# Value products of batch 0 on two column tiles of the array

## The chip, the cores and the metric

The kernel runs on one core of one Trainium2 chip. The metric is the device time of one execution in microseconds (us). TensorE (PE) does the matrix products; VectorE (DVE), ScalarE (ACT) and GpSimd (POOL) work elementwise; SyncE (SP) issues most of the DMAs. PEld names PE's loads of the stationary operand, which stand in rows of their own.

## The reference

Attention with a decay, for 8 batches and 8 heads of 576 tokens with 64 channels, and then a feed-forward layer with a softplus over all 4608 tokens.

```python
scores = scale * np.matmul(q, k.transpose(0, 1, 3, 2))
cum = np.cumsum(np.log(np.clip(f, 0.0001, 1.0)), axis=-1)
scores = np.where(causal, -1000000000.0, scores + cum[:, :, :, None] - cum[:, :, None, :])
attn = np.exp(scores - np.max(scores, axis=-1, keepdims=True))
attn = attn / (np.sum(attn, axis=-1, keepdims=True) + 1e-09)
x = np.matmul(attn, v)                     # 8 x 8 x 576 x 64, then 4608 x 512
h = x @ w_in                               # 512 -> 2048
g = np.maximum(h, 0.0) + np.log1p(np.exp(-np.abs(h)))
out = g @ w_out                            # 2048 -> 512
```

## The kernel before, in words

The program is one long list of operations that a planner (class Plan) puts in order. Each operation names the engines that may do it with a cost in us, what it comes after, and the buffers that it takes. The planner walks through the list with a clock for each engine, takes whatever can start first, and lets the engine with the better end do it. So a changed cost, or an operation split or merged, can change the order of the neighbours and the engine on which a copy runs. The order is fixed when the program is built; on the chip each engine works down its own list and waits where a semaphore tells it to.

Until the first product of the down projection (tile "acc") the planner also writes filler matmuls for PE (tile "fill", function fill_gap, line 1377): wherever its clock sees PE idle for more than 0.5 us it puts in matmuls of 128 columns for 0.7 of that time. They compute nothing that is used. They are instructions like others, and PE works through them whether or not it would have waited.

Attention goes job by job. Batch 0 is "plain": float32 operands, with one matmul in the program being two records in the trace. Its jobs are four pairs of heads for queries 0 to 255 (function first) and then eight single heads for queries 256 to 575 (function rest). All other batches (function whole) split each operand into a high and a low part and take two or three matmuls (lines 763, 764 and 918). A plain job computes scores (line 761, tile s), minima on DVE (line 768), exponentials on ACT (line 788), normalises, turns the weights with PE transposes (line 859, tile b), copies them out of PSUM (tile p; ACT or DVE), and multiplies them with the values (line 912, tile o). The output lies transposed: 64 channels on the partitions, queries in the columns, so the stationary operand is 128 keys by 64 channels and half of the array's columns are used. A copy by ACT or DVE then puts it into x, the feed-forward layer's input; that is the helper's line 213, as are all copies.

The value products are made by output(gi), one call for each range of queries and head in "groups". A pair has two groups, one for each head: two products each (256 and 128 columns) into a PSUM bank of their own. A single head has one group of 320 queries and five products, with 320, 320, 320, 192 and 64 columns, since the later keys are seen by the later queries only. In a list "banks" stand the parts of the turned weights: each entry is a first key, a range of queries and a chunk of v.

Weights arrive as 64-bit numbers and are converted in the first 150 us by ACT, POOL and DVE (lines 441 to 465), then split into high and low parts (lines 508 to 534). Block 0 of the feed-forward layer, 256 tokens, is also plain (lines 1057 and 1180); later blocks use lines 1076 and 1161. All PSUM banks of the attention come from one tag, "att", with four buffers.

Of the kernel before, what the change touches and what calls it, by code (L numbers as in the profile page):

```python
# [216 lines left out]
def tile_decay_attention_softplus_ffn(  # L217
# [18 lines left out]
    B, D, H, _, S = qkT.shape  # L236
    NT, DM = out.shape
    DFF = w_in.shape[1]
    P = 128
# [41 lines left out]
    T = {}  # L281
# [288 lines left out]
    def rest(h):  # L570
        return dict(
            b=0, heads=[h], q=(256, S), k=(0, S), nv=NCH,
            tiles=[(q0, n, 0, 2 + i, 0) for i, (q0, n) in enumerate(QR)],
            banks=[[(0, 256, S, 0), (384, 384, S, 3)], [(128, 256, S, 1), (512, 512, S, 4)],
                   [(256, 256, S, 2)]],
            groups=[(256, S, h, 256)],
        )

    x_of, x_taken = {}, {}
# [6 lines left out]
    def attention(job):  # L586
# [237 lines left out]
        def weights(bi):  # L824
# [70 lines left out]
            for key, lo, hi, vc, at in spans:  # L895
                parts.append((lo, hi, bi, vc, at, box, ready, small))

        def output(gi):
            g0, g1, h, tok = groups[gi]
            g, j = h // 2, h % 2  # L900
            todo = sorted(
                (p for p in parts if p[0] < g1 and p[1] > g0), key=lambda p: (max(p[0], g0) > g0, p[2])
            )
            box, last = {}, []
            for i, (lo, hi, bi, vc, at, pbox, ready, small) in enumerate(todo):
                a, z = max(lo, g0), min(hi, g1)

                def values(e, i=i, a=a, z=z, vc=vc, o=at + a - lo, pbox=pbox, xs="h" if small else "hl"):
                    if i == 0:
                        box["ps"] = bank("att", f"o{n}_{gi}")  # L910
                    if plain:
                        e.matmul(  # L912
                            box["ps"][0:64, a - g0 : z - g0], st["vr"][:, vc, :],
                            pbox["p"][:, o : o + z - a], start=i == 0, stop=i == len(todo) - 1,
                        )
                        return
                    for x in xs:
                        e.matmul(  # L918
                            box["ps"][:, a - g0 : z - g0], st["vhl"][:, vc, :],
                            pbox[x][:, o : o + z - a],  # L920
                            start=i == 0 and x == "h", stop=i == len(todo) - 1 and x == xs[-1],
                        )

                on = on_pe32(z - a) if plain else on_pe(z - a, len("h" if small else "hl"))
                op = add(
                    on, values, after=ready + last + st["V"],
                    takes=("att",) if i == 0 else (),
                )
                last = [op]
                used[bi].append(op)  # L930
            st.setdefault("ends", []).extend(last)
            w = g1 - g0


            def to():
                if b not in x_of:
                    x_of[b] = buf("x32", [P, NCC, S], f"x32_{b}")
                return x_of[b][64 * j : 64 * j + 64, g, tok : tok + w]

            def shift(e):  # L940
                copy(e, to(), box["ps"][64 - 64 * j : 128 - 64 * j, 0:w])

            def put(e):
                if plain:
                    copy(e, to(), box["ps"][0:64, 0:w])
                    return
                e.tensor_add(to(), box["ps"][64 * j : 64 * j + 64, 0:w], to())

            needs = last + x_taken.get(b, [])
            takes = () if b in x_taken else ("x32",)  # L950
            if plain:
                d = c = add([on_act(w, psum=True), on_dve(w)], put, after=needs, takes=takes)
            else:
                c = add(on_act(w, psum=True), shift, after=needs, takes=takes)
                d = add(on_dve(w), put, after=[c])
            x_taken.setdefault(b, [c])
            puts = [d]
            wrote.setdefault(b, []).append((tok, tok + w, d))
            give("att", puts)
            if gi == len(groups) - 1:  # L960
                if plain:
                    give("T0", st["scores"])
                    if number == nplain - 1:
                        give("x32", cum_used)
                    give(st["vtag"], st["ends"])
                    for bi, ops in used.items():
                        give(tags[bi], ops)
                else:
                    give("T", st["scores"])
                    give("vhl", st["ends"])  # L970
                    for bi, ops in used.items():
                        if banks[bi][0][:3] == (0, 0, 64):
                            give("ph64", ops)
                        else:
                            give("ph", ops)
                            give("pl", ops)

        def loads():
            (load32 if plain else load)()
# [3 lines left out]
            load=loads, prepare=None if plain else prepare, fin=finish_stats,  # L983
            s=[lambda ti=ti: stat_tile(ti) for ti in range(nt)],
            w=[lambda bi=bi: weights(bi) for bi in range(len(banks))],
            o=[lambda gi=gi: output(gi) for gi in range(len(groups))],
        )


# [481 lines left out]
```

## Time and profile before

| what | before |
|---|---|
| time, median of 3 runs | 1186.32 us (1185.65 to 1186.48) |
| profiled execution, its own time | 1184.87 us |
| its span, first to last instruction | 1183.1 us |
| granted clock of TensorE, mean | 0.999 |
| busy: PE, DVE, ACT, POOL | 1170.2, 809.2, 832.3, 131.0 us |
| value products of batch 0 (line 912) | 112 records, from 18.6 to 141.0 us |
| first "acc" product (line 1180) | 82.06 us |

The span is what the views show; the execution's own time has 1.8 us around it. Rows of PE overlap: the printed length of a matmul holds the time that its result takes to leave the array, so the cost of a row in a stream is read from its start to the next start. That PE is 99% busy therefore doesn't mean that PE streams columns for 99% of the time.

### The profile page before, as it was taken

How to read it: one execution, taken by the hardware profiler on the slowest of the kernel's cores; microseconds unless marked ns; L12 is line 12 of the kernel's file. 1: busy time of each engine (PE TensorE's matmuls, PEld its weight loads, DVE VectorE, ACT ScalarE, POOL GpSimd, SP SyncE). 2: the span in 40 equal slices, each digit the busy share in tenths (PEclk: the TensorE clock that was granted, in tenths of full speed). 3: DMA queues.
4: the chain of work that ended last, by engine and by line, in shares of the span. 5: the costliest groups of instructions: out<-in, count | busy, mean ns of one | idle time of the engine just before them, and what ended most of it. 6: DMA issues, size and time to landing. Idle time of an engine off the chain costs nothing.

```text
span 1183.1 us, 19397 instructions
## 1 busy us (share of the span) xinstructions
PE 1170.2 (99%) x6112; PEld 967.3 (82%) x6112; DVE 809.2 (68%) x2013; ACT 832.3 (70%) x1991; POOL 131.0 (11%) x145
## 2 busy tenths in 40 slices
PE   8999999999999999999999999999999999999998
PEld 6766678888888888888888888888888888888887
DVE  7977898987787678767776678667866773223322
ACT  5887779877876787677867877778767773444543
POOL 5312011100110011110000101001011010000000
PEclk9999999999999999999999999999999999999999
DMA  8856756655566555655566546656566433211210
GB/s 243 242 163 180 205 155 180 152 147 147 155 181 186 165 152 166 181 177 158 150 198 187 151 138 202 178 147 172 152 185 175 139 106 120 89 47 44 89 54 36
DMA packets 120759, 180.30 MB, mean 152 GB/s; under 512 B 22945, under 2 KB 80305, under 8 KB 120657
## 3 DMA queue, kind: packets, MB, share of 16 engines
q1 hardware_dynamic: 120640, 179.05, 52.9%
q8 instruction: 49, 0.80, 0.3%
q14 instruction: 54, 0.43, 0.1%
q10 hardware_dynamic: 16, 0.01, 0.0%
HBM read 109.98 MB, written 35.95 MB: 123 GB/s over the span
## 4 chain that ended last, share of the span: by engine, by line
PE 90%; DVE 5%; ACT 2%; issue 1%; DMA 1%; POOL 0%; SPq 0%; DVEq 0%; POOLq 0%; ACTq 0%
PE acc L1161 30%; PE h L1076 30%; PE b L859 8%; PE o L918 6%; PE s L764 3%; PE s L763 3%; PE h L1057 2%; PE acc L1180 2%; PE o L912 2%; PE s L761 1%; DVE s L768 1%; ACT p L788 1%; DMA sti<-in_w_in 1%; DVE pl L878 1%; DVE h L1123 0%
## 5 line engine op out<-in xcount | busy, mean ns | idle before, releaser
L1076 PE MATMUL h<-xh,wih 128*128 128x512 f32 (+1 forms) x576 | 228.9, 400 | 0.2 <-DVE gl L1131 0.2
L788 ACT ACTIVATE p<-s,negm 128x288 f32<-128x288 f32 (+7 forms) x384 | 183.0, 479 | 64.6 <-DVE negm L768 62.6
L1076 PE MATMUL h<-xl,wih 128*128 128x512 f32 (+1 forms) x576 | 216.5, 379 | 0.0
L768 DVE CUSTOM_DVE_ANT_0 s<-s,cmask 128x288 f32<-128x288 f32 (+5 forms) x320 | 137.7, 439 | 89.0 <-PE s L764 82.5
L1123 DVE SCALAR_TENSOR_TENSOR h<-h,e 128x512 f32<-128x512 f32 x136 | 95.7, 704 | 129.1 <-ACT e L1115 128.2
L812 POOL TENSOR_SCALAR p<-p,rsum 64x64 f32<-64x64 f32 (+4 forms) x83 | 91.7, 1113 | 759.9 <-DVE rsum L801 329.4
L1109 ACT ACTIVATE e<-h 128x512 f32<-128x512 f32 x144 | 85.9, 597 | 118.8 <-PE h L1076 115.8
L1161 PE MATMUL acc<-woh_dt_float32r,gh 128*128 128x512 f32 x376 | 153.2, 407 | 0.0
L1076 PE MATMUL h<-xh,wl 128*128 128x512 f32 (+1 forms) x576 | 148.6, 380 | 0.0
L1161 PE MATMUL acc<-woh_dt_float32r,gl 128*128 128x512 f32 x376 | 147.2, 392 | 0.0
L1161 PE MATMUL acc<-wol_dt_float32r,gh 128*128 128x512 f32 x376 | 146.9, 391 | 0.0
L878 DVE TENSOR_TENSOR pl<-b,ph 128x512 fp32r<-128x512 f32 x168 | 110.9, 665 | 19.6 <-ACT ph L213 16.3
L1131 DVE TENSOR_TENSOR gl<-h,gh 128x512 fp32r<-128x512 f32 x136 | 93.5, 687 | 42.7 <-ACT gh L213 40.3
L1076 PEld LDWEIGHTS h<-xh,wl 128*128 128x128 f32 x576 | 104.8, 188 | 21.5
L1076 PEld LDWEIGHTS h<-xh,wih 128*128 128x128 f32 x576 | 108.7, 189 | 15.4 <-PE b L859 0.4
L1076 PEld LDWEIGHTS h<-xl,wih 128*128 128x128 f32 x576 | 108.8, 189 | 14.5
L859 PE MATMUL b<-ident,p 128*128 128x128 f32 (+1 forms) x728 | 118.3, 270 | 1.1 <-POOL p L812 0.6
L213 ACT CAST ph<-b 128x512 fp32r<-128x512 f32 (+2 forms) x170 | 82.7, 487 | 47.9 <-PE b L859 40.9
L213 ACT CAST gh<-h 128x512 fp32r<-128x512 f32 x111 | 65.2, 587 | 57.4 <-DVE h L1123 38.0
L810 ACT ACTIVATE p<-p,rsum 128x192 f32<-128x192 f32 (+7 forms) x193 | 96.6, 555 | 6.1 <-DVE rsum L801 5.8
L859 PEld LDWEIGHTS b<-ident,p 128*128 128x128 f32 (+1 forms) x728 | 86.7, 138 | 16.4 <-issue 3.5
L763 PE MATMUL s<-T 128*64 128x64 f32 x336 | 97.6, 303 | 1.2 <-issue 1.1
(152 smaller groups left out, 2248.5 us busy)
## 6 DMA issues: line engine op xcount, KB each, us to landing
wl<-wil_d SPq DMA_DIRECT2D x72, 512.0 KB
T<-T SPq DMA_DIRECT2D x224, 144.0 KB
raw<-in_qkT SPq DMA_DIRECT2D x112, 144.0 KB
g_d<-gh SPq DMA_DIRECT2D x84, 128.0 KB
g_d<-gl SPq DMA_DIRECT2D x84, 128.0 KB
vr<-in_vR SPq DMA_DIRECT2D x64, 160.0 KB
out<-ob SPq DMA_DIRECT2D x36, 256.0 KB
sto<-in_w_out SPq DMA_DIRECT2D x11, 512.0 KB
```

The lines of the kernel that those rows point to most:

```text
L213: (e.tensor_copy if hasattr(e, "tensor_copy") else e.copy)(out, in_)
L763: e.matmul(o, qA[:, q0:end], kA[:, a:z], start=True, stop=False)
L768: e.tensor_tensor_reduce(out=box["o"], in0=box["o"], in1=cmask[0:n_q, right - w : right], scale=-0.125, scalar=m0 if i else 3.0e38, op0=AL ...
L788: e.activation(o, box["o"], AF.Exp, bias=m1, scale=-1.0, accum_out=acc)
L810: e.activation(a, a, AF.Copy, scale=f_)
L812: e.tensor_scalar(a, a, f_, None, ALU.mult)
L859: e.transpose(box["ps"][0 : x.shape[1], at : at + one.shape[1]], x, one)
L878: e.tensor_sub(box["l"], box["ps"][:, 0:w], box["h"].bitcast(F32))
L1076: e.matmul(o, l, r, start=m == 0, stop=m == 11)
L1123: e.scalar_tensor_tensor(h, h, 0.0, box["e"], ALU.max, ALU.add)
L1131: e.tensor_sub(box["l"], box["t"], box["h"].bitcast(F32))
L1161: e.matmul(st["acc", tt], l, r[fc], start=first and m == 0, stop=last and m == 2,)
```

## The change

A new function, output_tiled, takes the place of output(gi) in all plain jobs. The result of a job is put into one PSUM bank, with its first group on partitions 0 to 63 and its second on partitions 64 to 127; tile_position=(0, 64 * r) puts the stationary operand of group r into the left or the right 64 columns of the array. In a pair the two groups are the two heads. A single head gets two groups, queries 256 to 447 and 448 to 575. The products of both groups are written in turns and form one planner operation for each step (a step is a product of both heads in a pair, and a part of the turned weights in a single head), whose cost is counted as that of the wider group alone. A pair is copied out by one copy of 128 partitions, a single head by two copies of 64 partitions. output(gi) loses its plain branches.

```diff
@@ -573,7 +573,7 @@
             tiles=[(q0, n, 0, 2 + i, 0) for i, (q0, n) in enumerate(QR)],
             banks=[[(0, 256, S, 0), (384, 384, S, 3)], [(128, 256, S, 1), (512, 512, S, 4)],
                    [(256, 256, S, 2)]],
-            groups=[(256, S, h, 256)],
+            groups=[(256, 448, h, 256), (448, S, h, 448)],
         )
...
@@ -895,6 +895,75 @@
+        def output_tiled():
+
+            todo = []
+            for g0, g1, *_ in groups:
+                here = [x for x in parts if x[0] < g1 and x[1] > g0]
+                todo.append(sorted(here, key=lambda x: (max(x[0], g0) > g0, x[2])))
+            if pair:
+                steps = [[[x] for x in both] for both in zip(*todo)]
+            else:
+                steps = [[[x for x in ts if x[2] == bi] for ts in todo] for bi in range(len(banks))]
+            box, last, left = {}, [], [len(ts) for ts in todo]
+            for i, step in enumerate(steps):
+                mms, need, cols = [], [], []
+                for r, (ts, (g0, g1, *_)) in enumerate(zip(step, groups)):
+                    cols.append(0)
+                    for k, (lo, hi, bi, vc, at, pbox, ready, _) in enumerate(ts):
+                        a, z = max(lo, g0), min(hi, g1)
+                        left[r] -= 1
+                        mms.append((k, r, a - g0, z - g0, vc, pbox, at + a - lo, i + k == 0, not left[r]))
+                        cols[-1] += z - a
+                        need += ready
+
+                def values(e, i=i, mms=sorted(mms, key=lambda m: m[:2])):
+                    if i == 0:
+                        box["ps"] = bank("att", f"o{n}")
+                    for _, r, a, z, vc, pbox, o, start, stop in mms:
+                        e.matmul(
+                            box["ps"][64 * r : 64 * r + 64, a:z], st["vr"][:, vc, :],
+                            pbox["p"][:, o : o + z - a], start=start, stop=stop,
+                            tile_position=(0, 64 * r),
+                        )
+
+                op = add(
+                    on_pe32(max(cols)), values, after=need + last + st["V"],
+                    takes=("att",) if i == 0 else (),
+                )
+                last = [op]
+                for ts in step:
+                    for x in ts:
+                        used[x[2]].append(op)
+            st["ends"] = last
+
+            g, j = heads[0] // 2, heads[0] % 2
+            outs = [(0, P, *groups[0])] if pair else [(64 * r, 64, *x) for r, x in enumerate(groups)]
+            puts = []
+            for r, rows, g0, g1, _, tok in outs:
+                w = g1 - g0
+
+                def put(e, r=r, rows=rows, tok=tok, w=w):
+                    if b not in x_of:
+                        x_of[b] = buf("x32", [P, NCC, S], f"x32_{b}")
+                    to = x_of[b][64 * j : 64 * j + rows, g, tok : tok + w]
+                    copy(e, to, box["ps"][r : r + rows, 0:w])
+
+                takes = () if b in x_taken else ("x32",)
+                d = add(
+                    [on_act(w, psum=True), on_dve(w)], put, after=last + x_taken.get(b, []), takes=takes,
+                )
+                x_taken.setdefault(b, [d])
+                puts.append(d)
+                wrote.setdefault(b, []).append((tok, tok + w, d))
+            give("att", puts)
+            give("T0", st["scores"])
+            if number == nplain - 1:
+                give("x32", cum_used)
+            give(st["vtag"], st["ends"])
+            for bi, ops in used.items():
+                give(tags[bi], ops)
+
...
@@ -908,12 +977,6 @@
                     if i == 0:
                         box["ps"] = bank("att", f"o{n}_{gi}")
-                    if plain:
-                        e.matmul(
-                            box["ps"][0:64, a - g0 : z - g0], st["vr"][:, vc, :],
-                            pbox["p"][:, o : o + z - a], start=i == 0, stop=i == len(todo) - 1,
-                        )
-                        return
...
-                on = on_pe32(z - a) if plain else on_pe(z - a, len("h" if small else "hl"))
+                on = on_pe(z - a, len("h" if small else "hl"))
...
@@ -983,7 +1032,7 @@
             w=[lambda bi=bi: weights(bi) for bi in range(len(banks))],
-            o=[lambda gi=gi: output(gi) for gi in range(len(groups))],
+            o=[output_tiled] if plain else [lambda gi=gi: output(gi) for gi in range(len(groups))],
         )
```

The change moves instructions, since the planner's costs and operations are others. Three places follow; a number at the end of a name is a buffer's.

PE, third pair of heads (o_0, o_1 and o are value products, p the turned weights, b transposes, fill the fillers, s scores), before:

```order
42 L912 MATMUL o_0_418<-p_0_402,vr_153 64x256
43 L912 MATMUL o_0_418<-p_0_402,vr_153 64x128
44 L859 MATMUL b_1_428<-ident,p_640_95 128x128 x3
45 L1377 MATMUL fill<-cmask 128x128 x3
46 L912 MATMUL o_1_445<-p_1_435,vr_153 64x256
47 L912 MATMUL o_1_445<-p_1_435,vr_153 64x128
48 L1377 MATMUL fill<-cmask 128x128 x3
```

and after:

```order
42 L859 MATMUL b_1_401<-ident,p_640_95 128x128 x3
43 L1426 MATMUL fill<-cmask 128x128 x4
44 L924 MATMUL o_420<-p_0_397,vr_153 64x256
45 L924 MATMUL o_420<-p_1_412,vr_153 64x256
46 L924 MATMUL o_420<-p_0_397,vr_153 64x128
47 L924 MATMUL o_420<-p_1_412,vr_153 64x128
48 L1426 MATMUL fill<-cmask 128x128 x11
```

The four products stand together, behind the transposes of both heads, and take turns.

PE, third single head of batch 0, the last one ahead of the first "acc", before:

```order
133 L859 MATMUL b_2_794<-ident,p_640_95 128x128
134 L912 MATMUL o_0_803<-p_0_780,vr_635 64x320
135 L912 MATMUL o_0_803<-p_1_798,vr_635 64x320
136 L912 MATMUL o_0_803<-p_2_805,vr_635 64x320
137 L912 MATMUL o_0_803<-p_0_780,vr_635 64x192
138 L912 MATMUL o_0_803<-p_1_798,vr_635 64x64
139 L1377 MATMUL fill<-cmask 128x128 x4
140 L761 MATMUL s_0_0_840<-T_72 64x320
```

and after:

```order
137 L761 MATMUL s_2_288_803<-T_73 128x288
138 L924 MATMUL o_808<-p_0_781,vr_642 64x192
139 L924 MATMUL o_808<-p_0_781,vr_642 64x128
140 L924 MATMUL o_808<-p_0_781,vr_642 64x64
141 L924 MATMUL o_808<-p_0_781,vr_642 64x128
142 L924 MATMUL o_808<-p_1_786,vr_642 64x192
143 L924 MATMUL o_808<-p_1_786,vr_642 64x128
144 L924 MATMUL o_808<-p_1_786,vr_642 64x64
145 L924 MATMUL o_808<-p_2_797,vr_642 64x192
146 L924 MATMUL o_808<-p_2_797,vr_642 64x128
147 L1426 MATMUL fill<-cmask 128x128 x13
148 L761 MATMUL s_0_0_867<-T_72 64x320
```

Five products became nine, and the filler behind them 13 rows' worth where there were 4. Behind the value products of the last pair the fillers number 36 (in four places) and were 21 (in six).

DVE, up to the weights of the last pair (wih and wil are high and low parts of w_in, negm the minima), before:

```order
106 L213 CAST wih<-woh_dt_float_326 128x512
107 L213 CAST wih<-woh_dt_float_449 128x512
108 L768 ISA s_2_288_497,negm_75<-s_2_288_497,cmask,negm_75 128x288
109 L768 ISA negm_75 128x1
110 L213 COPY x_0_282<-o_0_501 64x256
111 L213 COPY p_1_518<-b_1_512 128x384
```

and after, at the same place of the last pair (its second transposes wait for row 97):

```order
97 L812 TENSOR_SCALAR p_640_100<-p_640_100,rsum_90 128x256
98 L512 TENSOR_TENSOR wil_477<-woh_dt_float_216,wih 128x512
99 L768 ISA s_0_0_467,negm_75<-s_0_0_467,cmask 64x320
100 L768 ISA negm_75 64x1
101 L512 TENSOR_TENSOR wil_489<-woh_dt_float_256,wih 128x512
102 L465 SCALAR_TENSOR_TENSOR woh_dt_float_446<-ti_440,woh_dt_float_446 128x512
```

The copy of the turned weights has gone to ACT, and the two low parts of line 512, which stood ahead of the last pair's weights, stand behind them. From the first down product of the third block on (line 1161, row 951 of PE before and 978 now), PE's rows are the same in both programs.

More of the change, by code (lines that the diff above doesn't have):

```diff
@@ L943, in put @@
             def put(e):
-                if plain:
-                    copy(e, to(), box["ps"][0:64, 0:w])
-                    return
                 e.tensor_add(to(), box["ps"][64 * j : 64 * j + 64, 0:w], to())
@@ L950, in output @@
             takes = () if b in x_taken else ("x32",)
[L951 to L955, printed above, removed]
+            c = add(on_act(w, psum=True), shift, after=needs, takes=takes)
+            d = add(on_dve(w), put, after=[c])
             x_taken.setdefault(b, [c])
@@ L960, in output @@
             if gi == len(groups) - 1:
[L961 to L976, printed above, removed]
+                give("T", st["scores"])
+                give("vhl", st["ends"])
+                for bi, ops in used.items():
+                    if banks[bi][0][:3] == (0, 0, 64):
+                        give("ph64", ops)
+                    else:
+                        give("ph", ops)
+                        give("pl", ops)
         def loads():
```

## The prediction, made before the changed kernel ran

> **What bounds the kernel now.** First the page: the engines' busy time, the chain that ended last, and the group of the products that are edited.
>
> ```profile
> span 1183.1 us, 19397 instructions
> PE 1170.2 (99%) x6112; PEld 967.3 (82%) x6112; DVE 809.2 (68%) x2013; ACT 832.3 (70%) x1991; POOL 131.0 (11%) x145
> PE 90%; DVE 5%; ACT 2%; issue 1%; DMA 1%; POOL 0%; SPq 0%; DVEq 0%; POOLq 0%; ACTq 0%
> ```
>
> PE is busy all the time and the chain runs on it for 90% of the span. So PE time saved where PE is the chain shortens the kernel, one for one until another engine is late. The edited products end early, so the second view is the table of stretches, for all instructions and then for the filler matmuls alone (line 1377).
>
> ```profile
> 20.00:43.00 23.00, 21.46 (x123) 15.79 (x122) 22.44 (x59) 19.68 (x51) 11.05 (x14) 0.93 0.88 274
> 43.00:82.00 39.00, 38.97 (x202) 28.07 (x203) 34.11 (x92) 32.79 (x73) 7.96 (x10) 1.00 0.60 181
> 82.00:149.00 67.00, 67.00 (x288) 43.27 (x287) 53.76 (x132) 51.08 (x119) 11.69 (x13) 1.00 0.68 198
> 149.00:260.00 111.00, 108.56 (x693) 94.08 (x692) 101.08 (x278) 91.25 (x245) 14.90 (x13) 1.00 0.60 160
> 43.00:82.00 39.00, 5.97 (x42) 5.23 (x42) 1.00 0.60 181
> ```
>
> The columns are the stretch, its length, busy PE, PEld, DVE, ACT, POOL, granted clock, DMA share and GB/s. Until 43 us DVE is the full engine (22.44 of 23.00). From 43 us on PE has no idle time, but up to 82 us 42 of its 202 records are fillers. From 82 us there are none, and PE is full with work.
>
> The third view is the chain at the seam, the fourth the timeline of PE.
>
> ```profile
> 42.43 0.47 DVE p L213
> 42.95 0.86 PE o L912 x4
> ```
>
> ```profile
> 7.71 2.84 PE L1377 MATMUL fill<-cmask 128*128 128x128 f32 x24
> 10.39 2.92 PE L761 MATMUL s<-T 66*128 66x128 f32 x14
> ...
> 18.56 0.86 PE L912 MATMUL o<-p,vr 128*64 128x256 f32 x4
> 19.36 0.94 PE L1377 MATMUL fill<-cmask 128*128 128x128 f32 x6
> ...
> 62.43 2.27 PE L912 MATMUL o<-p,vr 128*64 128x320 f32 x10
> 64.63 1.16 PE L1377 MATMUL fill<-cmask 128*128 128x128 f32 x8
> ...
> 78.61 3.62 PE L1057 MATMUL h<-x,woh_dt_float 128*128 128x256 f32 x16
> 82.06 3.60 PE L1180 MATMUL acc<-wol_dt_float,g 128*128 128x512 f32 x8
> 85.49 0.65 PE L761 MATMUL s<-T 66*128 66x288 f32 x2
> ```
>
> The chain passes from DVE (a copy of turned weights) to PE with the last head pair's second value product at 42.95 us. A record's printed length contains its drain, so I cost by starts. Sixteen records of 256 columns take 82.06 - 78.61 = 3.45 us, 0.216 each; eight of 512 take 3.43, 0.429 each: 0.84 ns per column and record. A float32 product stands as two records (18.56: two products, x4).
>
> **The value products now.** One head of queries 256 to 575 has five products with 320, 320, 320, 192 and 64 columns: 1216 columns in two records each, 1216 x 2 x 0.84 ns = 2.04 us. The row at 62.43 takes 64.63 - 62.43 = 2.20 us. The rest, 0.16 us, is the way into and out of the 64-wide stationary form. Half a pair has 384 columns, 0.645 us, and takes 19.36 - 18.56 = 0.80: 0.155 again. There are eight such heads, three before 82 us and five behind:
>
> ```profile
> L912 PEld LDWEIGHTS o<-p,vr x50: 132/137/137, 86.1 to 140.9; 128*64 128x64 f32 x50
> L912 PE MATMUL o<-p,vr x50: 219/432/484, 86.1 to 141.0; 128*64 128x320 f32 x30, 128*64 128x192 f32 x10, 128*64 128x64 f32 x10
> ```
>
> **The value products after.** No row of this trace shows two column tiles at once, so the cost is bounded from both sides. The nine products of a head come in the order A192, B128, A64, B128, A192, B128, B64, A192, B128 (A is queries 256 to 447 on output partitions 0 to 63, B is 448 to 575 on 64 to 127), two records each.
>
> - No overlap: the same 1216 columns, 2.04 us, plus eight more records for the four products that the split adds. Nothing in the rows above asks more than a few ns for a record: 2.20 to 2.25 us a head, 0 to 0.05 lost.
> - Each tile busy without regard to order: the wider range of each of three steps, 256 + 192 + 192 = 640 columns, 1.075 + 0.155 = 1.23 us, 0.97 saved. This is what the planner's table now counts.
> - Between them, a record starts no earlier than the one ahead of it, and waits while its own tile streams. The two records of one product share a tile, so only the second record of A runs beside the first of B. With 0.161, 0.107 and 0.054 us for 192, 128 and 64 columns: A192 from 0 to 0.322; B128 from 0.161 to 0.376; A64 to 0.43; B128 to 0.59; A192 starts with B's second record at 0.484 and ends at 0.806; B128 to 0.86; B64 to 0.97; A192 from 0.914 to 1.236; the last B128 to 1.29. With 0.155 for the way in and out 1.45 us, 0.75 saved.
>
> I take the third, 0.75, because in no row that I read does a PE record overtake another. Eight heads: 8 x 0.75 = **-6.0 us**, 3.75 of it behind 82 us. For the four pairs (A256, B256, A128, B128) it gives A to 0.43, B from 0.215 to 0.645, A128 to 0.645, B128 to 0.86, with 0.155 1.0 us in place of 2 x 0.80. These lie before 43 us beside DVE's 22.44 of 23.00: counted at nothing; if DVE did not cover them they would be worth 4 x 0.6 = 2.4 us more. Of the last pair PE's own stretch from 42.95 holds the whole now and not the second half: **+0.2**.
>
> **Fillers.** They are code, fixed by the plan. Behind the last pair the order lists 3 + 8 + 12 + 13 = 36 rows of them, before 5 + 4 + 2 + 3 + 4 + 3 = 21, which are the 42 records above. The 24 records from 7.71 to 10.39 us cost 0.112 each, so 30 more records are +3.4; they stand in four places and not six, which takes away some ways in and out: **+3.2 us**. PE had no idle time around its fillers between 43 and 82 us, so I see nothing that they hide, and they count in full. If the other engines are late there anyway, they cost nothing and PE would have waited instead; the term is then between 0 and 3.2, and the saving of the three heads ahead of 82 us (2.25) goes with it. One scores product of two records (0.5 us) moves from behind the first "acc" to ahead of it: no net.
>
> **DVE before 43 us.** The rows for copies and weight work in the first 150 us:
>
> ```profile
> L213 DVE COPY p<-b 128x384 f32<-128x384 f32 x8 | 4.4, 549 | 0.5 <-PE b L859 0.5
> L512 DVE TENSOR_TENSOR wil<-woh_dt_float,wih 128x512 fp32r<-128x512 f32 x12 | 8.7, 723 | 0.0
> L213 DVE CAST wih<-woh_dt_float 128x512 fp32r<-128x512 f32 x8 | 4.2, 533 | 0.1
> L310 DVE MEMSET T<- 2x576 f32 x3 | 1.6, 538 | 0.9 <-PE s L761 0.6 <-issue 0.3
> L213 DVE COPY x<-o 64x320 f32<-64x320 f32 x5 | 2.4, 482 | 2.3 <-PE o L912 2.1
> L213 DVE COPY x<-o 64x256 f32<-64x256 f32 x3 | 1.2, 413 | 0.0
> ```
>
> Ahead of the last pair's weights the new order has two copies of turned weights fewer on DVE (ACT takes them), two low parts (line 512) later, one cast and one memset earlier: -1.1 - 1.4 + 0.5 + 0.5 = -1.5 us. ACT is busy 19.68 of 23.00 there and the DMA queues at 0.88, and they may set the end instead. So 0 to -2, and I take **-1.0**. The added wait is small: a pair's first product needs the weights of both heads, and what stands behind it on PE are transposes and scores of the next pair. With DVE as the bound this delays nothing that I can price; with 0.55 us for one weight copy it is at most 4 x 0.55 = 2.2 inside that stretch.
>
> **Copies out.** By the two copy rows a copy has (482 - 413) / 64 = 1.08 ns a column and 0.14 us besides. A head's 320 columns become 192 and 128: +0.14 us, five times behind 82 us, on DVE (53.76 of 67.00) or ACT (51.08). A pair's two copies become one, -0.41 us each. Behind the slack of both engines: 0. If that cover were gone, 0.7 us.
>
> **Whether the saving lasts.** Behind 82 us PE would need 67.0 - 3.75 - 0.5 = 62.8 us up to the same work, DVE 53.8 + 0.7: 87%. From 149 to 260 us DVE has 101.08 of 111.00, still under PE. Short waits of PE for DVE and ACT may come of it: **+0.5** (0 to 1.5). From the third block's first down product on (259 us before) PE's row order is the same in both programs, so I carry the shift to the end unchanged.
>
> Sum: -6.0 + 0.2 + 3.2 - 1.0 + 0.5 = **-3.1 us**, made against the profiled execution (span 1183.1, its own time 1184.87) and so 1181.8 there. The median of the three runs is 1186.32, 1.45 above it: **1183.2 us**.
>
> **The rivals**, each with the other terms kept:
>
> 1. Half overlap, as above: 1183.2; with its terms' bounds 1181.3 to 1185.3. 45%.
> 2. Both tiles always busy: 8 x 0.22 = 1.8 less, 1181.4. For it: loads of 64 columns leave PE's stream unbroken now (2.04 of 2.20). Against: in-order starts. 17%.
> 3. The change does not do what it says: the products run one behind another. The 6.0 is gone, the fillers stay: -3.1 + 6.0 = +2.9, and less late work behind means no +0.5: 1188.7. For it: no row with overlap. 17%.
> 4. Overlap, but each of the nine products shows part of its weight load. Price: from nothing to half of the way in and out, 0.078 us, which has such a load in it. At the middle, 0.04, 9 x 0.04 = 0.35 of the 0.75 goes, 8 x 0.40 = 3.2 is saved: 1186.0; at the end 1188.7. For it: a tile has to be loaded twice for each product. 10%.
> 5. Each change of tile breaks the stream. Place: the seven changes between A and B in a head. Price: half of the way in and out, 0.078, up to a whole load, 0.137 by the row above, and no overlap: 7 x 0.078 to 7 x 0.137 = 0.54 to 0.96 us lost a head. In the middle 8 x 0.75 = 6.0, with fillers, pair and DVE +8.4: 1194.7. It decides once a change costs more than the overlap gains, 0.75 / 7 = 0.107. Against it: the ten loads of a head, 0.137 each, would be 1.37 us, yet 2.20 - 2.04 leaves 0.16, so loads do run beside products. 11%.
>
> For the fifth, the Trainium skill, "TensorE: Matmul & The Clock Gate", Part 3 ("What overlaps and what doesn't"), says that a weight load overlaps a running matmul only where the row groups differ; column tiles share them, so by it the load at each change shows, and the time would be the upper end, 1196.4. The trace disagrees for one tile, by the 0.16 us just named. The same page's "Measured speedup vs the span model" gives 2.38 times for three column tiles (no run here shows it); shared out to two, 2.38 x 2 / 3 = 1.59, an estimate, a head would take 2.04 / 1.59 + 0.155 = 1.44 us, and the sum would stay as it is.
>
> **How the numbers follow.** Differences under 0.2% (2.4 us, so 1183.9 to 1188.7) can't be told from none. Of the first case's 45% some 31 fall below 1183.9 and 12 within; of the second 16 and 1; the third, at the edge, gives 8 within and 9 slower; the fourth 1, 8 and 1; the fifth 11 slower. That is 48% faster, 29% the same, 23% slower. The range 1180.5 to 1189.0 leaves out the fifth, the top of the third and a little under the second; the likeliest case alone has 1181.3 to 1185.3.
>
> **What would show it.** In the profile after: a head's nine products from first start to the next line's start in 1.45 us (1.23, 2.2, 1.9 or over 2.7 for the rivals), with records of A and B starting within a few ns of each other; 72 filler records behind the last pair; the first "acc" near 82 us (within 1.5); the third block's down products 3 us earlier than 259.5. Wrong would be: PE idle in front of products between 43 and 149 us, waiting for DVE or ACT, or a first "acc" later than 84 us.

## The result and the profile after

The change takes 1190.35 us (median of eight executions, 1187.01 to 1192.12) where the kernel before takes 1186.40 (1185.08 to 1188.75): 1.0031 times the time, with a 95% interval of 1.0022 to 1.0040. It is 0.31% slower, and the forecast said 3.1 us faster. The page of the changed kernel, with the engines' busy time, the granted clock in 40 slices and the chain of waits by engine:

```profile
span 1188.7 us, 19593 instructions
PE 1168.6 (98%) x6206; PEld 970.2 (82%) x6206; DVE 811.0 (68%) x2014; ACT 837.5 (70%) x1997; POOL 128.4 (11%) x142
PEclk9899999989999999999999999999999999999999
PE 86%; DVE 7%; ACT 4%; DMA 2%; issue 1%; SPq 0%; POOL 0%; DVEq 0%; ACTq 0%
```

PE is busy 1.6 us less than before, and the span is 5.6 us longer: the time went into waits. By the medians the loss is 4.0 us: the profiled execution of the kernel before, 1184.87 us, lies 1.5 under its median, that of the change, 1190.51, at its own. So differences between the two profiles show the loss some 1.7 us too large. The chain's share of PE is 4 points lower and that of DVE and ACT together 4 points higher. In slices 2 and 9 of PEclk (each 29.7 us long) the granted clock was below nine tenths.

The edited products themselves, in the timeline of PE (start, duration, line, operands, records):

```profile
22.84 0.87 PE L924 MATMUL o<-p,vr 128*64 128x256 f32 x8
23.64 0.94 PE L1426 MATMUL fill<-cmask 128*128 128x128 f32 x6
...
64.79 1.31 PE L924 MATMUL o<-p,vr 128*64 128x192 f32 x18
66.02 2.94 PE L1426 MATMUL fill<-cmask 128*128 128x128 f32 x24
```

A head's nine products take 66.02 - 64.79 = 1.23 us (2.20 before), and both heads of a pair together 0.80, as long as one of them took before. The overlap is complete: 640 columns at 0.84 ns in two records each are 1.075 us, and 0.155 go in and out of the 64-wide form. So a head saves 0.97 us, more than was forecast.

The stretches tell where it went (stretch, length, busy PE, PEld, DVE, ACT, POOL, granted clock, DMA share, GB/s). After:

```profile
43.00:82.00 39.00, 37.81 (x241) 28.33 (x238) 31.86 (x85) 31.00 (x72) 7.08 (x8) 0.95 0.56 165
82.00:149.00 67.00, 65.87 (x332) 44.05 (x331) 54.96 (x136) 51.61 (x117) 10.31 (x14) 1.00 0.70 197
149.00:230.00 81.00, 79.86 (x535) 70.61 (x534) 73.81 (x206) 69.42 (x184) 12.13 (x11) 1.00 0.62 165
230.00:260.00 30.00, 26.62 (x141) 22.25 (x140) 23.81 (x62) 20.89 (x59) 3.04 (x3) 0.89 0.42 109
```

and the last of them before:

```profile
230.00:260.00 30.00, 29.38 (x166) 24.93 (x165) 27.29 (x71) 23.30 (x64) 2.96 (x3) 1.00 0.59 156
```

Between 230 and 260 us all three engines do less than before, in less clock: PE lacks 3.38 us of 30 where it lacked 0.62, and does 25 matmuls fewer. Four marks in the profiled executions put the loss in order (us from the span's start; "acc" is the first down product, "block 3" the third block's first down product, behind which PE's rows are the same):

| | first "h" | first "acc" | block 3 | end | "acc" to block 3 |
|---|---|---|---|---|---|
| before | 44.96 | 82.06 | 259.49 | 1183.1 | 177.43 |
| change | 44.65 | 85.87 | 266.21 | 1188.7 | 180.35 |

The change reaches block 3 6.7 us late: 3.8 are lost ahead of the first "acc", and 2.9 behind it, though five heads save 4.85 there and a scores product of 0.5 has gone. Behind block 3 the rest is a microsecond shorter (922.5 against 923.6).

**Ahead of the first "acc".** PE after:

```profile
44.65 7.37 PE L1106 MATMUL h<-x,woh_dt_float 128*128 128x256 f32 x28
51.95 0.75 PE L761 MATMUL s<-T 66*64 66x320 f32 x2
...
85.87 3.60 PE L1229 MATMUL acc<-wol_dt_float,g 128*128 128x512 f32 x8
```

```profile
40.00:47.00 7.00, 6.54 (x22) 4.62 (x23) 6.08 (x19) 6.12 (x15) 1.81 (x2) 0.51 0.47 142
```

The clock was halved just when the first "h" products ran: 28 records took 51.95 - 44.65 = 7.30 us, where 28 x 0.216 would be 6.05. From the first "h" to the first "acc" it takes 41.2 us (37.1 before), 4.1 more. Thirty more filler records are 3.4, the scores product 0.5, the clock 1.25, idle PE 1.2 (39.00 - 37.81); the value products save 2.9. That makes 3.45 of the 4.1; the rest was not located. It is a sum of PE's rows and does not say what PE would have waited for without them; two experiments below show that fillers and the halved clock of this stretch are not what costs.

**Behind it.** The timeline of PE around 240 us; in brackets the idle time and what ended it:

```profile
240.48 0.31 PE L764 MATMUL s<-T 68*128 68x320 f32 x1
242.94 0.47 PE L763 MATMUL s<-T 128*128 128x448 f32 x1 [2.15 <-ACT p L788]
...
245.64 0.42 PE L981 MATMUL o<-ph,vhl 128*128 128x64 f32 x1 [0.98 <-DVE ph L875]
...
247.17 0.78 PE L1125 MATMUL h<-xh,wih 128*128 128x512 f32 x1
247.75 0.63 PE L1125 MATMUL h<-xl,wih 128*128 128x512 f32 x1
```

ACT and DVE ahead of it:

```profile
237.03 0.59 ACT L213 CAST ph<-b 128x512 fp32r<-128x512 f32 x1 [2.65 <-PE b L859]
```

```profile
237.16 0.46 DVE L213 CAST T<-raw 128x576 fp32r<-128x576 f32 x1 [1.31 <-PE s L763]
```

and the chain of waits in this place (start, us, what):

```profile
233.61 2.83 PE acc L1210 x12
...
247.52 2.56 PE h L1125 x6
...
252.92 1.41 PE h L1125 x6
```

```profile
245.00:252.00 7.00, 6.23 (x20) 5.39 (x21) 5.42 (x13) 2.66 (x8) 0.00 (x0) 0.51 0.11 25
```

Twelve down products in a row leave ACT and DVE without work (2.65 and 1.31 us idle). Twelve attention matmuls and six more down products later, 28 attention matmuls stand in a row with no feed-forward product between them; they need ACT and DVE all along, and PE waits 2.15 and 0.98 us (and 1.12 once more up to 261.0 us, behind this stretch). From 245.0 us on the clock is halved for 6.8 us, and six "h" products take 2.56 us that take 1.41 five microseconds later. In the order of PE after, the run of 28 is this:

```order
874 L1210 MATMUL acc_1_1910<-woh_dt_float32r,gl_7_2750 128x512
875 L981 MATMUL o_1_2775<-ph_3_2773,vhl_2346 128x320
...
885 L763 MATMUL s_3_0_2831<-T_1352 128x448
...
901 L859 MATMUL b_3_2871<-ident,p_640_95 128x128 x2
902 L1125 MATMUL h_0_2879<-xh_2625,wih 128x512
```

Before, the longest such run between feed-forward products is 15 matmuls. The last edited product starts at 147.6 us; here only the planner's order has changed.

### The profile page after: what moved, and what is told of

It reads as the page before. It is cut to its first block, busy times and chain, and to the rows that moved or that the text cites. A ratio compares the mean times of both kernels' runs of the same rounds, so it can differ in the third digit from the quotient of the medians.

```text
span 1188.7 us, 19593 instructions
## 1 busy us (share of the span) xinstructions
PE 1168.6 (98%) x6206; PEld 970.2 (82%) x6206; DVE 811.0 (68%) x2014; ACT 837.5 (70%) x1997; POOL 128.4 (11%) x142
## 4 chain that ended last, share of the span: by engine, by line
PE 86%; DVE 7%; ACT 4%; DMA 2%; issue 1%; SPq 0%; POOL 0%; DVEq 0%; ACTq 0%
PE acc L1210 30%; PE h L1125 30%; PE b L859 7%; PE o L981 6%; PE s L764 3%; PE s L763 3%; PE h L1106 2%; PE acc L1229 2%; ACT p L788 1%; DVE s L768 1%; DVE pl L878 1%; DMA sti<-in_w_in 1%; PE s L761 1%; PE o L924 1%; ACT p L810 1%
## 5 line engine op out<-in xcount | busy, mean ns | idle before, releaser
L812 POOL TENSOR_SCALAR p<-p,rsum 128x192 f32<-128x192 f32 (+4 forms) x81 | 90.6, 1126 | 764.9 <-DVE rsum L801 366.1
L1180 DVE TENSOR_TENSOR gl<-h,gh 128x512 fp32r<-128x512 f32 x136 | 93.6, 688 | 41.2 <-ACT gh L213 38.7
L213 ACT CAST ph<-b 128x512 fp32r<-128x512 f32 (+2 forms) x170 | 83.0, 490 | 46.9 <-PE b L859 41.2
L810 ACT ACTIVATE p<-p,rsum 128x576 f32<-128x576 f32 (+6 forms) x195 | 97.9, 558 | 5.6 <-DVE rsum L801 5.0
```

What stands on the lines that cost most here:

```text
L213: (e.tensor_copy if hasattr(e, "tensor_copy") else e.copy)(out, in_)
L810: e.activation(a, a, AF.Copy, scale=f_)
L812: e.tensor_scalar(a, a, f_, None, ALU.mult)
L1180: e.tensor_sub(box["l"], box["t"], box["h"].bitcast(F32))
```

## The experiments

The first theory was that the overlap works and the planner's new order gives more back than it gains: the first cost that changes in the planner's table moves everything behind it. The rivals were that the overlap is worth nothing on the path, and that the thirty more fillers are the loss. Each ratio stands against executions of the kernel before on the same chip; differences from the change are between medians of different chips, on which the kernel before has 1186.08 to 1186.40 us.

**The planner's cost as before, products as in the change.**

```diff
-                    on_pe32(max(cols)), values, after=need + last + st["V"],
+                    on_pe32(sum(cols)), values, after=need + last + st["V"],
```

> Both column tiles as in the change, but the planner counts a step at the columns of both groups together, as it did before the change. The order is then near that of before: 24 rows of fillers behind the last pair (the change 36, before 21). Theory (the products do overlap, 1.23 us a head in place of 2.20; what was lost is the new order with its fillers, waits and the halved clock): 8 x 0.97 = 7.8 us less than before, 0.7 more for three rows of fillers, up to 3 us of it lost to waits: 1179 to 1183 us. Rival (the tiles themselves cost time elsewhere, by the clock or by waits that any faster product brings): 1187 to 1192, as the change.

Measured: 1187.27 us, 1.0005 (0.9996 to 1.0013), no difference from before and 3.1 us less than the change. The same operations with another number in the planner's table, from which order and fillers follow: 3.1 of the 4.0 us of loss go with that number. But the theory's range was missed by 4 us, and the figure lies inside the rival's, at its lower end: the loss goes and no gain comes. The profile can't tell why, since its execution (1184.26 us) is the second fastest of twelve, 3 us under the median; its 174.95 us from "acc" to block 3 show what this order can reach, and not what it takes as a rule. Why this order gains nothing stays open.

**The change's order, without the overlap.** Pairs stay as in the change; a single head's five products run whole on one column tile, and the two copies take their columns from there.

```diff
+                    if not pair:
+                        whole_ = list({x[3]: x for ts in step for x in ts}.values())
+                        for k, (lo, hi, _, vc, at, pbox, _, _) in enumerate(whole_):
+                            e.matmul(box["ps"][0:64, lo - 256 : hi - 256], st["vr"][:, vc, :],
+                                pbox["p"][:, at : at + hi - lo], start=i + k == 0, ...)
+                        return
...
-                    copy(e, to, box["ps"][r : r + rows, 0:w])
+                    r0, c = (r, 0) if pair else (0, 3 * r)
+                    copy(e, to, box["ps"][r0 : r0 + rows, c : c + w])
```

> The change's order on every engine, its planner costs, fillers and copies, but a single head's products stand on one tile again, as the five products of before; the pairs keep both tiles. Theory (the overlap is worth 0.97 us a head on PE's path): eight heads take 2.20 us again, 5 x 0.97 = 4.9 us more behind the first down product and up to 2.9 ahead of it: 1194 to 1198 us. Rival (in this order PE waits for others anyway, so the saving had turned into waits): 1189 to 1192.

Measured: 1195.63 us, 1.0083 (1.0069 to 1.0096), 5.3 us more than the change. In its timeline of PE a head takes 66.97 - 64.77 = 2.20 us again:

```profile
64.77 2.27 PE L926 MATMUL o<-p,vr 128*64 128x320 f32 x10
66.97 2.94 PE L1436 MATMUL fill<-cmask 128*128 128x128 f32 x24
```

So in one and the same order the overlap is worth 5.3 of its 8 x 0.97 = 7.8 us, as the theory had it. By the marks below, 3.8 of it come behind the first "acc", where five heads make 4.85, and 0.5 ahead of it, where three make 2.9. The gain is real, and something else costs more.

**No fillers behind the last pair**, in the change and then in the kernel before (all 72 records of the one and all 42 of the other are gone):

```diff
-                if "acc" in op.takes:
+                if "acc" in op.takes or ("h" in op.takes and self.port[1] > 20):
                     self.fill = None
```

> The change without the 72 filler records behind the last pair, all else in the same order. Theory (fillers are work on PE's path): up to 72 x 0.112 = 8.1 us less, with waits of PE taking some of it back: 1183 to 1187 us. Rival (the fillers cover waits for ACT and DVE that are there anyway): 1189 to 1192; or the longer idle time halves the clock once more, 1190 to 1194.

> The kernel before without its 42 filler records behind the last pair, all else in the same order. Theory (they are on PE's path, since PE had no idle time around them): 42 x 0.112 = 4.7 us less than before, or somewhat less: 1181.7 to 1184 us. Rival (they cover waits): 1185.5 to 1187.

Measured: the change without them 1193.95 us, 1.0066 (1.0054 to 1.0079), 3.6 us slower than with them; the kernel before 1186.15, 1.0000 (0.9991 to 1.0009). Both theories fell; in the change it is the rival with the halved clock that held, in the kernel before the one with the waits. The stretches show why, for the change first and then for the kernel before:

```profile
62.00:79.00 17.00, 15.10 (x63) 9.84 (x62) 10.61 (x30) 11.88 (x28) 2.96 (x4) 0.50 0.32 90
```

```profile
43.00:82.00 39.00, 35.61 (x167) 23.15 (x166) 35.60 (x96) 33.81 (x75) 8.89 (x10) 1.00 0.60 182
```

Without fillers PE of the kernel before is idle for 3.39 of 39 us, and its first "acc" comes at 82.23 where it came at 82.06: its fillers stood in waits and cost nothing. So PE does not set the end of this stretch in the order of before, and PE time saved in it is worth nothing there. In the change the clock stays halved for 17 us when they are gone. That the fillers are the loss is refuted in this form: they can't simply be taken out. What thirty more of them cost beside that, this pair can't tell; the run with 0.05 below can.

**Before's order, with the overlap.** The planner, its operations and its table are those before; each product of a single head is written as two parts on two tiles, and the copy as two copies in one operation.

```diff
+                    if plain and not pair:
+                        for t, (c0, c1) in enumerate(((256, 448), (448, S))):
+                            u, w = max(a, c0), min(z, c1)
+                            if u < w:
+                                e.matmul(box["ps"][64 * t : 64 * t + 64, u - c0 : w - c0], ...,
+                                    tile_position=(0, 64 * t))
+                        return
```

> The kernel before, with its planner costs, operations and so its order on every engine; only the five products of a single head are each written as one or two products on two column tiles, and the copy out of a head is two copies one behind the other on the engine that had the one. The pairs are as before. Theory (the overlap is good and the new order is what lost): no gain ahead of the first down product, where the run of before without late fillers showed that PE waits for others; five heads behind it at up to 0.97 us each, less 5 x 0.14 for copies and some waits: 1182 to 1184 us. Rival (what PE saves behind the first down product turns into waits for ACT and DVE, whatever the order): 1185.5 to 1187.

Measured: 1183.89 us, 0.9979 (0.9970 to 0.9988): 2.3 us faster than before. The order decides the sign. That is what the theory said. But of 4.85 us behind the first "acc" only half arrives (by the marks, "acc" to block 3 takes 175.92, 1.5 less). PE between 85 and 140 us, in the stretches for PE alone, here and then before:

```profile
85.00:140.00 55.00, 53.27 (x284) 1.00 0.71 199
```

```profile
85.00:140.00 55.00, 55.00 (x236) 1.00 0.67 195
```

1.73 us of the saving are idle PE in the very stretch where it arises. 1.41 of them are one wait, up to 132.13 us: PE's first scores product of the next batch (line 763) waits for a DMA into tile T. So a transfer was late next.

**Pairs alone, and heads alone.**

```diff
-            o=[output_tiled] if plain else [...],
+            o=[output_tiled] if pair else [...],                 # pairs alone
+            o=[output_tiled] if plain and not pair else [...],   # heads alone
```

> Only the pairs are made as in the change; single heads have the products, the group and the planner cost of before. Of the change's order this keeps the start, up to the first single head, and has 28 rows of late fillers; from row 430 of PE on it is the order of before. Theory (the pairs take work from PE where it is already waiting, the clock is halved around 40 us and the first down product comes 2 to 4 us late): 1187 to 1190 us. Rival (the pairs do nothing, the loss comes with the single heads' new costs): 1185.5 to 1187.

> Only the single heads are made as in the change; the pairs are as before, and so is the order up to the first single head. 28 rows of late fillers; PE's order is another than before's up to row 980. Theory (the loss behind the first down product, PE idle and the clock halved near 245 us, comes with the single heads' planner costs): if that wait stays, 1186 to 1190 us; if it goes away with the pairs' shift, the five heads' gain shows, 1181 to 1184.

Measured: pairs alone 1186.19 us, 1.0002 (0.9994 to 1.0011); heads alone 1183.71, 0.9978 (0.9969 to 0.9987). The first is the rival's figure, the second the theory's for the case that the wait goes away. Neither part is slower: 0 and -2.5 us alone, +4.0 together. The jobs of the two parts are different ones, and what they share is the planner's order.

**Fillers ahead of the last pair, against the halved clock at 40 us** (before that pair, gaps above 0.15 us are filled whole):

```diff
-                elif op.start - clock["PE"] > 0.5:
-                    self.fill(engines["PE"], 0.7 * (op.start - clock["PE"]))
+                elif op.start - clock["PE"] > (0.5 if self.filled else 0.15):
+                    self.fill(engines["PE"], (0.7 if self.filled else 1.0) * (op.start - clock["PE"]))
```

> The change, with fillers ahead of the last pair put in for every planned gap over 0.15 us and for all of it (58 records more), all else in the same order. Theory (PE's idle time between 24 and 42 us halves its clock from 40 to 47 us, 2.4 us of which fall on work behind the last pair, 1.2 us lost): no halving there, 1188 to 1189.5 us. Rival (that halving is hidden behind ACT and DVE): 1190 to 1191; fillers in the way of work: 1191 to 1193.

Measured: 1190.90 us, 1.0038 (1.0025 to 1.0050), the same as the change, as the rival had it. The early halving was gone, and the first "acc" came 0.6 us earlier, at 85.30; the time did not follow. The later halving stayed, as its stretches for PE alone show:

```profile
230.00:245.00 15.00, 11.96 (x72) 0.99 0.46 126
245.00:260.00 15.00, 14.30 (x67) 0.78 0.37 89
```

So the halved clock at 40 us is no cause of the loss; the place around 240 us is left.

**The change, with 0.05 and 0.08 us more for each step in the planner's table.** Nothing else is altered; the operations are the same.

```diff
-                    on_pe32(max(cols)), values, after=need + last + st["V"],
+                    On("PE", on_pe32(max(cols)).cost + 0.05), values, after=need + last + st["V"],
```

> The change with 0.05 us more in the planner's cost of each two-tile step, which brings a head to what it was measured at (1.23 us). Nothing else is edited; the order changes. 37 rows of late fillers (the change 36); the 28 attention matmuls in a row with no feed-forward product among them, at which PE stood idle near 240 us in the change, are gone (the longest row behind the first down product is 19, and that is its first). Theory (the loss behind the first down product is that one place in the order): about 5 us under the change, 1184 to 1187 us. Rival (the late first down product and the tiles are the loss, in any order): 1189 to 1191.

> The change with 0.08 us more for each two-tile step: another order, 33 rows of late fillers, no more than 14 attention matmuls in a row. Theory: 1182 to 1186 us. Rival: 1189 to 1191.

Measured: 1182.20 us, 0.9969 (0.9959 to 0.9980), and 1181.63 us, 0.9959 (0.9947 to 0.9971): 8.2 and 8.7 us less than the change, and faster than before. Stretches, with 0.05 and then 0.08:

```profile
230.00:260.00 30.00, 29.76 (x170) 25.43 (x169) 27.44 (x73) 23.95 (x61) 3.66 (x3) 1.00 0.52 144
```

```profile
230.00:260.00 30.00, 29.77 (x168) 25.43 (x167) 27.80 (x73) 24.11 (x61) 3.66 (x3) 1.00 0.51 146
```

Both are lower than the theory's ranges. The run of 28 is gone (the longest are 19 and 14), PE is busy for 29.8 of 30 us at full clock, and "acc" to block 3 takes 174.33 and 174.92 us: 6.0 and 5.4 less than in the change, 3.1 and 2.5 less than before. With 0.05 the first "acc" still comes at 85.19, with 74 late filler records; with 0.08 the clock is halved for 6.8 us around 40 us as in the change. So the late first "acc", the fillers and the early halving were there and the kernels were faster all the same: none of the three is the loss. What is left is the stall around 240 us. That is by exclusion, for the new number moves other operations too: no run takes the stall alone out of the change's order.

**Heads alone, with 0.12 us more, and with the full cost.**

```diff
-                    on_pe32(max(cols)), values, ...
+                    On("PE", on_pe32(max(cols)).cost + 0.12), values, ...
+                    on_pe32(sum(cols)), values, ...
```

> Single heads alone on two tiles, the pairs as before, and 0.12 us more for each two-tile step: 25 rows of late fillers (with heads alone and no such addition 28), no more than 16 attention matmuls in a row. Theory (the nearer the plan stays to what the products take, the less waits): 1182 to 1184 us. Rival (the waits behind the first down product stay, whatever the order): as with heads alone, 1183 to 1185.

> Single heads alone on two tiles, the pairs as before, and each step counted at the columns of both groups: 22 rows of late fillers and an order near that of before. Theory: like the run with before's own order, 1182.5 to 1184.5 us. Rival (the split into two copies in the plan costs): 1185 to 1187.

Measured: 1183.92 us, 0.9979 (0.9971 to 0.9988), and 1185.66, 0.9999 (0.9990 to 1.0007). The first is equal to heads alone, which fits theory and rival alike. The second loses its gain, at the rival's figure, though its profile shows no stall (but that execution, 1183.73 us, is the fastest of eleven). So a higher number is not better by itself, and with the full cost both programs gain nothing, for a reason that no run here shows. With the heads overlapped, all that was tried lies between 1181.6 and 1194.0 us, and the best is the change with 0.08.

The marks of those orders that bear on this, beside those above:

| | first "acc" | block 3 | end | "acc" to block 3 | clock halved, 230 to 260 us |
|---|---|---|---|---|---|
| full cost | 84.10 | 259.05 | 1182.4 | 174.95 | no |
| change's order, one tile | 86.41 | 270.52 | 1192.9 | 184.11 | 6.8 us |
| change, no late fillers | 88.89 | 270.90 | 1193.4 | 182.01 | 6.8 us |
| change, early fillers | 85.30 | 265.82 | 1189.3 | 180.52 | 6.8 us |
| before's order, two tiles | 82.73 | 258.65 | 1182.0 | 175.92 | no |
| cost + 0.05 | 85.19 | 259.52 | 1182.0 | 174.33 | no |
| cost + 0.08 | 84.20 | 259.12 | 1181.6 | 174.92 | no |

Every program with the change's order here has the stall and the clock halved behind it, and only these are slower than before beyond the noise; no other program here has both. Heads alone has shorter waits in that place, 2.23 us in all between 230 and 260 us and none over 0.74, at full clock, and is 2.5 us faster than before. These are marks of one execution each; those of "full cost" and of the kernel before lie 3.0 and 1.5 us under their medians.

## Why the prediction was wrong

**What held.** The trace's reading of PE as the bound behind the first "acc" held in the main (in the change's order 3.8 us of 4.85 come and go with the overlap there), 72 late fillers were there, and the third, fourth and fifth rival fell with the first timeline: the products do overlap, no weight load shows, and a change of tile breaks no stream. By the Trainium skill, "TensorE: Matmul & The Clock Gate", Part 3 ("What overlaps and what doesn't"), the loads of column tiles would have shown; 18 loads and 18 records in 1.23 us disagree.

**"I take the third, 0.75"** (the value products): 0.97, the second rival's figure. The reason given, that no record overtakes another, was no evidence, since no row of one tile could show it. This error was on the good side, and not the cause.

**"Eight heads: -6.0"**: three of them lie where PE does not set the end. There the prediction went by "PE had no idle time around its fillers ..., so I see nothing that they hide, and they count in full". That step failed: without fillers the kernel before takes the same time with 3.39 us of idle PE. A filler row is idle time that the planner expected, and PE's 38.97 busy of 39.00 said nothing on who was late. The alternative stood there ("PE would have waited instead"), with no chance of its own. The first "acc" then came at 85.87, beyond the 84 that was named as a sign against.

**"Whether the saving lasts: +0.5 (0 to 1.5)"**: this is the step that turned the sign. From the first "acc" to block 3 it said 3.75 + 0.5 - 0.5 less, and 2.9 more was measured. It took the new order for the old one with a shift, and priced short waits from the engines' shares. The planner instead made one new place, at 233 to 252 us, some 85 us behind the last edited product, with which some 6 us go (180.35 against 174.33 with 0.05 more in the table): 3.14 us more of idle PE (29.76 - 26.62), and a clock halved for 6.8 us, at most 3.4 more. How the 6 divide between the two was not separated: the halving comes behind the waits in every program that has the stall. Part of the gain is lost without any stall too, as 1.73 us of idle PE with before's order show.

**"DVE before 43 us: -1.0"**: the first "h" came 0.31 earlier; the pairs, "counted at nothing", are worth nothing alone (1.0002); "Copies out: 0" was not separated. All are small beside the rest.

The forecast figure, 3.1 us faster, is close to what the overlap gives in an order without the stall (2.2 to 4.5 us faster in five of them, nothing in the two with the full cost), but it has parts of both signs in it that are wrong. No rival had this mechanism, an order made worse far from the edit by a changed cost, though the order of both programs was at hand: a run of 28 attention matmuls against 15 could have been counted.

## What to carry to other kernels

Where a planner sets the order, a correct saving is one term and the order that it produces is another, and the second can be larger: read the new order up to the point where both programs are the same again, look for the longest stretch of one kind of work on the bounding engine, and price what starves behind it. Small offsets of the changed cost (here 0.05 and 0.08 us) are cheap trials that tell a bad order from a bad change, and here they gave the best kernel. Fillers on the bounding engine can mark time in which that engine is not the bound (here 42 records could go and nothing was gained); a saving beside them is best counted at nothing until a run without them says otherwise.

## What the runs showed of the hardware

Two column tiles ran independently, in float32 with two records for a product: the first records of both tiles start within 7 ns of each other (64.788 and 64.795 us), and the 128-column tile's second record starts at 64.955, ahead of the 192-column tile's second at 65.002: a record waits for its own tile and not for the other. A 1216-column head in 1.23 us for 2.20 is 1.79 times, and without the 0.155 us in and out 1.9 times.

The clock was halved not only with PE idle but behind stretches in which it was busy for seven to eight tenths, as in the two of the change that run up to the halvings and a little into them:

```profile
235.00:246.00 11.00, 7.87 (x48) 6.55 (x46) 8.86 (x25) 7.65 (x21) 1.08 (x1) 0.95 0.36 92
24.00:42.00 18.00, 14.66 (x90) 10.41 (x90) 17.26 (x44) 15.01 (x36) 8.45 (x10) 0.95 0.89 263
```

Away from the end of the span it lasted 3.4, 6.8 or 17.1 us in these runs, which are one, two and five times 3.41. It isn't the same in all executions of a kernel: of the change's eight, six had a mean clock of 0.994 (1188.85 to 1192.12 us) and one 0.997 (1187.01 us, 3.3 under the median). Since 6.8 us at half clock are 0.003 of the span, a halving of that length seems to be absent in that execution; which one, and whether the 3.3 us are its price, a single execution can't tell. With 0.05 more in the table the clock was between 0.997 and 1.0, and the executions lay between 1180.20 and 1187.01 us. The profiled one of that kernel took 1183.78, above its median, so its marks understate it.
